# The last 224 rows of w_out: two transfers to sixteen partitions instead of four to eight

## The chip, the cores and the metric

One core of a Trainium2 chip runs the whole program. The metric is the device time of one execution in microseconds (us), as the median of several executions. Executions of one kernel mostly agree within 0.3 us, at most 0.65.

## The reference

For four tokens `x` (4 x 640) it computes `x + A(layernorm(x)) + B(layernorm(x))`. A is attention with a cache of 32 heads and 4096 keys for each token; B is a gated MLP.

```python
q = (xn @ wq)                                  # 640 -> 32 heads x 128
p = softmax(q . k_cache * Dh**-0.5)            # k_cache, v_cache: 4 x 32 x 4096 x 128, bf16
A = (p . v_cache) @ wo                         # 4096 -> 640
z = gelu(xn @ w_in)                            # 640 -> 2 x 864
B = (z1 * (layernorm(z2) * w_sp + b_sp)) @ w_out   # 864 -> 640
```

The two caches are 268 MB of the 282 MB that are read. Each element is used once, so the kernel is a long stream from memory.

## The kernel before

The loads are issued from the sync engine's queue in a fixed order: wq, w_in, the first 640 rows of w_out on 128 partitions, then the last 224 rows of w_out ("the rows" from here on), then units of K and V of 8.39 MB each (K0, K1, ...), and wo last. The rows lie on partitions 0 to 31, seven rows of w_out (8,960 bytes) on each, because the matmul that uses them contracts over those 32 partitions. Where a transfer is called one of "eight rows" or "sixteen rows", a row is what one partition gets: seven rows of w_out, one packet of 8,960 bytes.

```python
wq = at_slot(0, n_q)...;   nc.sync.dma_start(out=wq, in_=A_wq...)          # 5.24 MB
w_in = at_slot(2, n_in)...; nc.sync.dma_start(out=w_in, in_=B_w_in...)      # 2.21 MB
w_out = at_slot(2, FA * NOUT, n_in)...
nc.sync.dma_start(out=w_out, in_=B_w_out[0:nf, :]...)                       # 0.82 MB
w_rest_t = ktpool.tile([P, NKT], F32, tag="kT", name="w_rest")
w_rest = w_rest_t[:32].bitcast(BF16)[:, 0:FR * NOUT].rearrange("p (c n) -> p c n", c=FR)
w_rest_d = B_w_out[nf:Fh, :].rearrange("(i r c) n -> r i c n", r=4, c=FR)
for r in range(4):
    nc.sync.dma_start(out=w_rest[r:32:4], in_=w_rest_d[r])                  # 8 rows, 72 KB
# ... cut ...
load_unit(seq[0])                                                           # K0
```

Transfer r fills partitions r, r + 4, ..., r + 28.

Of the kernel before, what the change touches and what calls it, by code (L numbers as in the profile page):

```python
# [16 lines left out]
def kernel(  # L17
# [19 lines left out]
    nc = tc.nc  # L37
# [18 lines left out]
    Fh = F2 // 2  # L56
    FA = 5
    FR = (Fh - FA * P) // 32
# [56 lines left out]
    nf = FA * P  # L115
# [3 lines left out]
    w_rest = w_rest_t[:32].bitcast(BF16)[:, 0:FR * NOUT].rearrange("p (c n) -> p c n", c=FR)  # L119

    NB = 32 * FC
    z_at = n_in + FA * NOUT
    w_rest_d = B_w_out[nf:Fh, :].rearrange("(i r c) n -> r i c n", r=4, c=FR)
    for r in range(4):
        nc.sync.dma_start(out=w_rest[r:32:4], in_=w_rest_d[r])


    seq = [("k", u) for u in range(B)]
# [212 lines left out]
    for fc in range(FC):  # L341
        n = P if fc < FA else 32
# [248 lines left out]
```

## Time and profile before

| | before |
|---|---|
| median time (first 3 runs) | 664.21 us (664.03 to 664.24) |
| span in the profile | 662.5 us |
| read from memory | 282.25 MB, 426 GB/s over the span |
| K0 complete on all engines | 43.38 us |
| last slice of wo: first and last engine | 654.50 and 658.98 us |

The last two rows come from the completion records in the trace: a transfer over 128 partitions leaves sixteen and each of the four small ones eight. I read that as one from each DMA engine that takes part (K0's first packets start in sixteen streams, at 21.59 to 23.38 us, and K0 leaves sixteen records). The kernel is a stream on sixteen DMA engines that hardly idle (DMA share 1.00 from 30 to 620 us), so the useful question about a load is not "who waits for it" but "which engines does it put back, by how much, and are those the ones that finish last". The prediction shows and reads the lines of the page.

### The profile page before, as it was taken

To read this page: it belongs to the slowest core of one execution; us is meant where nothing else is said; L and a number is where in the kernel's file an instruction comes from. 1 tells how busy PE (TensorE), PEld (TensorE's weight loads), DVE (VectorE), ACT (ScalarE), POOL (GpSimd) and SP (SyncE) were. 2 spreads that over 40 slices of the span, in tenths; PEclk is the share of its full clock that TensorE was granted. 3 is DMA by queue.
4 is the path that set the end of the run, shared out by engine and by line. 5 is a ranking of instruction groups with operands and counts; after the bars stand their busy time and mean duration, and the time that the engine had idled before them with its cause. 6 is when DMAs were issued, how large, how long until landed. Compare 5 with 4: busy or idle time off the path is not lost.

```text
span 662.5 us, 5421 instructions
## 1 busy us (share of the span) xinstructions
PE 292.9 (44%) x2297; PEld 106.5 (16%) x2297; DVE 360.1 (54%) x275; ACT 78.4 (12%) x162; POOL 20.3 (3%) x64
## 2 busy tenths in 40 slices
PE   0636666256072556225336054533506254623245
PEld 0111122112021122111112022111202112211122
DVE  2249899556191759618256286745619185951112
ACT  0300000530100000530200000071010000053200
POOL 6210000000000000000000000000000000000000
PEclk9858768678577587677859596756958759667767
DMA  9999999999999999999999999999999999999996
GB/s 371 463 424 427 426 444 437 435 436 416 443 432 423 439 418 442 433 439 440 423 420 435 432 421 452 433 424 431 431 436 444 428 431 415 445 432 437 418 419 262
DMA packets 6901, 282.61 MB, mean 427 GB/s; under 512 B 808, under 2 KB 1084, under 8 KB 1468
## 3 DMA queue, kind: packets, MB, share of 16 engines
q1 hardware_dynamic: 6856, 282.25, 98.8%
q8 instruction: 18, 0.29, 0.2%
q14 instruction: 7, 0.06, 0.0%
q10 hardware_dynamic: 20, 0.01, 0.0%
HBM read 282.25 MB, written 0.01 MB: 426 GB/s over the span
## 4 chain that ended last, share of the span: by engine, by line
DMA 74%; DVE 11%; issue 11%; PE 2%; ACT 1%; SPq 0%; DVEq 0%; ACTq 0%
DMA kv<-in_A_k_cache_dram 64%; DVE kT L367 11%; DMA kv<-in_A_v_cache_dram 5%; DMA kv<-in_A_wo_dram 3%; DMA kv<-in_A_wq_dram 2%; PE O L449 2%; ACT xd L432 0%; ACT Zb L413 0%; ACT p L421 0%; DVE pT L425 0%; PE last_a L553 0%; DVE m L385 0%; PE S L378 0%; SPq L169 0%; PE misc L390 0%
## 5 line engine op out<-in xcount | busy, mean ns | idle before, releaser
L367 DVE STREAM_TRANSPOSE kT<-kv 128x2048 f32<-128x2048 f32 x128 | 282.8, 2276 | 124.7 <-DMA kv<-in_A_k_cache_dram 124.7
L378 PE MATMUL S<-kT,QZ 128*32 128x512 bf16 x1024 | 187.9, 500 | 230.6 <-DVE kT L367 230.6
L378 PEld LDWEIGHTS <-QZ 128*32 128x32 bf16 x1024 | 60.3, 111 | 353.4 <-issue 332.6
L449 PE MATMUL O<-kv,Zb 128*32 128x512 bf16 x1024 | 73.6, 451 | 58.2 <-DMA kv<-in_A_v_cache_dram 38.0
L458 DVE TENSOR_TENSOR om<-O,Mk 128x512 f32<-128x512 f32 x15 | 10.4, 692 | 109.0 <-PE O L449 109.0
L413 ACT ACTIVATE Zb<-xd,MkE 32x256 bf16<-32x256 bf16 x116 | 52.9, 498 | 110.4 <-PE O L449 109.0
L421 ACT ACTIVATE p<-S,negmax 128x512 bf16<-128x512 f32 x8 | 5.4, 683 | 400.6 <-DVE negmax L399 400.6
L449 PEld LDWEIGHTS <-Zb 128*32 128x32 bf16 x1024 | 32.9, 112 | 97.4 <-issue 55.8
L472 PE MATMUL misc<-R,SelR 128*32 128x128 f32 x32 | 6.4, 281 | 30.0 <-DVE R L459 28.4
L353 POOL COPY QZ<-qT 32x32 bf16<-32x32 bf16 x16 | 5.1, 318 | 390.6 <-PE S L378 389.9
L432 DVE COPY xd<-pT 32x256 bf16<-32x256 bf16 x44 | 16.0, 365 | 0.8
L459 DVE TENSOR_REDUCE R<-om 128x128 f32<-128x512 f32 x15 | 15.3, 1019 | 0.5
L432 ACT COPY xd<-pT 32x256 bf16<-32x256 bf16 x20 | 12.3, 614 | 5.6 <-DVE pT L425 5.2
L425 DVE STREAM_TRANSPOSE pT<-p 128x1024 bf16<-128x1024 bf16 x4 | 5.0, 1245 | 6.3 <-ACT p L421 6.3
L472 PEld LDWEIGHTS misc<-R,SelR 128*32 128x32 f32 x32 | 2.2, 107 | 37.8 <-DVE R L459 26.0
L385 DVE TENSOR_REDUCE m<-S 128x2 f32<-128x1024 f32 x4 | 4.9, 1225 | 5.5 <-PE S L378 5.5
L274 PE MATMUL q<-kv,xnT 128*32 128x512 bf16 x40 | 4.5, 630 | 6.9 <-DMA kv<-in_A_wq_dram 6.9
L461 DVE TENSOR_SCALAR R<-O,Mk 128x128 f32<-128x128 f32 x1 | 0.4, 351 | 12.5 <-PE O L449 12.5
L282 DVE CAST kv<-q 128x512 bf16<-128x512 f32 x1 | 0.7, 692 | 11.1 <-PE q L274 11.1
L390 PE MATMUL misc<-dg,ones_f 128*128 128x256 f32 x8 | 3.2, 488 | 7.6 <-DVE dg L387 7.6
L475 DVE SCALAR_TENSOR_TENSOR om<-misc,rinv,SelH 32x1024 bf16<-32x1024 f32 x4 | 5.1, 1271 | 2.0 <-PE misc L472 2.0
L437 PE MATMUL misc<-rowsum,SelPe 128*32 128x1 f32 x16 | 2.1, 202 | 9.0 <-ACT p L421 9.0
(102 smaller groups left out, 78.2 us busy)
## 6 DMA issues: line engine op xcount, KB each, us to landing
kv<-in_A_k_cache_dram SPq DMA_DIRECT2D x8, 4096.0 KB
kv<-in_A_v_cache_dram SPq DMA_DIRECT2D x1, 6144.0 KB
kv<-in_A_wq_dram SPq DMA_DIRECT2D x1, 5120.0 KB
kv<-in_A_wo_dram SPq DMA_DIRECT2D x3, 1280.0 KB
kv<-in_B_w_in_dram SPq DMA_DIRECT2D x1, 2160.0 KB, 19.9
kv<-in_A_v_cache_dram SPq DMA_DIRECT2D x1, 2048.0 KB
kv<-in_B_w_out_dram SPq DMA_DIRECT2D x1, 800.0 KB
kv<-in_A_wo_dram SPq DMA_DIRECT2D x1, 640.0 KB, 22.0
```

What stands on the lines that cost most here:

```text
L353: nc.gpsimd.tensor_copy(out=QZ[r0:r0 + 32, :, :, :, 8 + 8 * hp], in_=qT[32 * g:32 * g + 32, NE * hp:NE * hp + NE].rearrange("p e a b -> p ...
L367: nc.vector.transpose(kT[:].rearrange("p (t r) -> p t r", r=32), kw)
L378: nc.tensor.matmul(S_ps[32 * q:32 * q + 32, e], lhsT=QZ[:, b, 2 * kh + w, e, w0:w0 + 32], rhs=kb[:, i, :, e, :, w], start=(b == 0 and k < ...
L413: nc.scalar.activation(out=dst, in_=src, func=ACT.Copy, scale=mk)
L421: nc.scalar.activation(out=p_bf[:, :, e, :], in_=S_ps[:, e], func=ACT.Exp, bias=negmax[:, e:e + 1], scale=scale, accum_out=rowsum[:, e:e + 1])
L425: nc.vector.transpose(pT[:].rearrange("p t h x -> p (t h x)"), p_bf[:].rearrange("p t e m -> p (t e m)"))
L432: op(out=xd[32 * hp:32 * hp + 32, :, q, :], in_=pT[32 * q:32 * q + 32, :, hp, :].rearrange("p t x -> p x t"))
L449: nc.tensor.matmul(O_ps[32 * q:32 * q + 32, :, :], lhsT=Zb[b % 2][:, w].rearrange("p h c -> p (h c)"), rhs=vv[:, w * 4 * Dh:(w + 1) * 4 * ...
L458: nc.vector.tensor_tensor(out=om4[:], in0=O_ps[:], in1=Mk4[:, :, None].to_broadcast((P, 4, Dh)), op=ALU.mult)
L459: nc.vector.tensor_reduce(out=R, in_=om4[:].rearrange("p c d -> p d c"), axis=AX.X, op=ALU.add)
L472: nc.tensor.matmul(oh[:], lhsT=SelR[:, b].rearrange("p h b -> p (h b)"), rhs=state["R"][:, b, :], start=(b == 0), stop=(b == B - 1))
L475: nc.vector.scalar_tensor_tensor(out=om[:], in0=oh[:, None, :].to_broadcast((G, HG, Dh)), scalar=state.pop(("rinv", g))[:, 0:1], in1=MkH[: ...
```

## The change

The intent: eight rows use eight of the sixteen engines (eight completion records for each transfer in the trace of before); sixteen rows use all sixteen, and the eight no longer fall behind the others.

```diff
-    w_rest_d = B_w_out[nf:Fh, :].rearrange("(i r c) n -> r i c n", r=4, c=FR)
-    for r in range(4):
-        nc.sync.dma_start(out=w_rest[r:32:4], in_=w_rest_d[r])
+    w_rest_d = B_w_out[nf:Fh, :].rearrange("(i r c) n -> r i c n", r=2, c=FR)
+    for r in range(2):
+        nc.sync.dma_start(out=w_rest[r:32:2], in_=w_rest_d[r])
```

Bytes, rows and their places stay the same. A transfer now fills every second partition instead of every fourth.

## The prediction

What no trace or run of this case shows is cut from the recorded texts, here and under the experiments, and the cuts are marked. The sum of the prediction came to -0.6 us, so to 663.6, all of it from step 2. Between that and the 664.1 to 664.4 of rival (b) the forecast is 663.8. For (b), that a packet takes about twice 0.338 us, the times that follow, and that it is as likely as (a), stand as my estimates. For the range the runs of before (within 0.21 us) and rival (d) remain; the rest of its width is my estimate.

"Lower eight" and "upper eight" are names for the eight engines that carry the rows before the change and the eight that do not; the trace gives no numbers of engines. That the four transfers use the same eight is read from the two groups of K0 starts; that eight-row transfers use these eight in the other runs too is assumed. The order of issue, by the last record of each load: wq 15.92 us, w_in 21.03, w_out 22.93, the rows 23.72, K0 43.38. The completions of all loads fall on eight semaphores, and the fourth piece's eight records (23.28 to 23.72 us) on that of wq.

> **What bounds the kernel now.** I read the page first, then the windows, the DMA queue's waits, the chain of waits, the DMA view of the microseconds that hold the changed transfers, and last the packet records one by one. The page:
>
> ```profile
> DVE  2249899556191759618256286745619185951112
> DMA  9999999999999999999999999999999999999996
> GB/s 371 463 424 427 426 444 437 435 436 416 443 432 423 439 418 442 433 439 440 423 420 435 432 421 452 433 424 431 431 436 444 428 431 415 445 432 437 418 419 262
> ...
> q1 hardware_dynamic: 6856, 282.25, 98.8%
> q8 instruction: 18, 0.29, 0.2%
> ...
> DMA 74%; DVE 11%; issue 11%; PE 2%; ACT 1%; SPq 0%; DVEq 0%; ACTq 0%
> ```
>
> The reader is to see that the DMA row is full in 39 of 40 slices while the fullest compute engine, DVE, has many slices at 1 or 2. One queue (q1) fills 98.8% of the time of sixteen DMA engines with 282.25 MB. The chain names DMA for 74%; its 11% of DVE is the turn in which a finished K unit is transposed before its buffer is reloaded, and it runs while the queue still has other units to move. The windows say this more sharply (their last two figures are DMA share and GB/s):
>
> ```profile
> 2.00:22.00 20.00, 5.74 (x56) 2.36 (x57) 4.58 (x10) 2.05 (x3) 9.04 (x32) 1.00 0.96 410
> 62.00:640.00 578.00, 257.34 (x2020) 93.69 (x2015) 329.63 (x240) 71.01 (x152) 3.91 (x13) 0.73 1.00 432
> 640.00:659.00 19.00, 10.16 (x120) 4.46 (x121) 4.15 (x9) 0.00 (x0) 0.00 (x0) 0.68 0.85 354
> 659.00:662.50 3.50, 0.45 (x4) 0.08 (x1) 0.67 (x2) 0.00 (x0) 0.00 (x0) 0.50 0.01 1
> ```
>
> From 62 to 640 us the share is 1.00. The packet records agree: each 64 KB packet takes 2.418 us, on each engine the next starts at once, and an 8.39 MB unit passes every 19.35 us, while the issue view gives 29.7 us from issue to landing: some 10 us of earlier work is always queued ahead. So the engines are never waited for by themselves, and the end is set by the engine that is furthest behind. From 640 to 659 us the share falls to 0.85 because the engines finish apart: in the records the completions of one transfer are spread over 2.1 us at the first K unit and about 4.5 us at the last slice of wo. The last 3.5 us are matmuls, adds and the store after the last landing.
>
> The part that the change touches is small, but a wait in it is not:
>
> ```profile
> SPq L125 <- DMA kv<-in_A_wq_dram: 11.5, 1, 11.5
> ...
> 0.73 15.19 DMA kv<-in_A_wq_dram
> ...
> 15.94 0.62 SPq L125
> ...
> 16.60 26.78 DMA kv<-in_A_k_cache_dram
> ```
>
> The first line is a wait of the DMA queue, the others are pieces of the chain (start, length). The fourth eight-row transfer cannot be issued until wq has landed at 15.9 us, and the first K unit, K0, waits behind it in program order and is issued at 16.60. The built program tells why: there are eight completion semaphores for these loads, and the fourth piece takes the one that wq still uses.
>
> [...]Eight rows give 8 engines, sixteen give 16. The trace of before agrees: each of these four transfers leaves eight completion records, a 128-row load sixteen; and K0 starts on eight engines at 21.59 to 22.62 us and on the other eight at 22.94 to 23.38. [...]The trace agrees (wq, w_in, w_out, these rows and K0 pass in the order of issue).[...]
>
> **The change part by part.** Removed: two transfers of the four. Bytes, rows and destinations stay: 32 packets of 8,960 bytes, 0.287 MB of 282. No compute instruction changes; what differs on PE, DVE, ACT and GpSimd is numbering of buffers.
>
> 1. Balance. Each packet takes 0.338 us in the records. Before, each of the lower eight engines carries 4, so 4 x 0.338 = 1.35 us; the upper eight carry none. That is just the step between the two groups of K0 starts. After, all sixteen carry 2, 0.68 us. The lower eight come out 0.68 us earlier, the upper eight 0.68 us later.
>
> 2. What this is worth at the end. As no engine idles, a shift at 22 us is carried to 659 us. The other large disturbances are instruction fetches of 16 KB (18 in the page), each of which I see put one engine back by about 1.47 us (at 41.3 us: 1.00 us before the next packet could start and 0.46 us in that packet). At the last slices the completions lie, from the first, at about 2.7 to 2.9, 3.2, then 4.3, 4.4, 4.4 and 4.7 us. The last four fit lower engines hit twice: 1.35 to 1.79 plus 2 x 1.47 gives 4.3 to 4.7. An upper engine hit twice stands at 2.9 to 3.5 (0 to 0.55 plus 2.94). After: lower 3.6 to 4.0, upper 3.6 to 4.2. So the last engine comes 0.5 to 0.7 us sooner, call it 0.6. I cannot follow single engines through the trace with certainty (where two are level they can be swapped), so this attribution is an estimate.
>
> 3. The wait. With two pieces fewer, nothing of this group needs a semaphore in use by wq; K0 needs only the one of the small load of x, which landed at about 3.2 us. So K0 is issued at 3.4 to 4 us rather than 16.60, and the 11.5 us wait goes. Worth: K0's first packet ran at 21.59 us, 5.0 us after its issue, because w_in, w_out and these rows were ahead of it. The early issue only lengthens the queue. K1 still waits for wq's place to be free (the copy of q, at 23.1 us), K2 for K0's transposes. Value 0.
>
> 4. Sequencer: two issues fewer, 2 x 0.62 us, hidden too: 0. The later loads have the same waits with other semaphore numbers, and the consumer of these rows runs at 36.7 us against a landing near 23: 0.
>
> Sum: -0.6 us of 664.21, giving 663.6 if the engines alone set the rate.
>
> **The rivals.**
> (a) Engine-bound, as summed: 663.6. For it: the steady 2.418 us for 64 KB on all engines (27.1 GB/s each) and the exact 1.35 us step.
> (b) [...]a packet takes about twice 0.338 us, the lower eight need 1.35 us as before and the upper eight fall back by 1.35. The slowest (lower, 4.7) stays where it is; upper ones reach 2.9 to 3.5 plus 1.35, about 4.9 at worst. Time 664.1 to 664.4. [...]against it nothing in the trace. I hold this about as likely as (a).
> (c) The 11.5 us wait is on the path, and several us are won: 655 to 660. For it: the chain passes through it (wq, L125, K0). Against it: the 5.0 us that K0's first packet stands queued, and a DMA share of 0.96 in the first window[...]. I give it 1 in 100.
> (d) The engine that ends last is one of the upper eight, or the fetches fall on other engines in the new run: up to 0.7 us slower, or one fetch, 1.5 us, either way. 664.9 to 665.7 at worst.
>
> **Range and chances.** Weighing (a) and (b) equally gives 663.9; with a little for the gain side, because a packet may be shared at less than full contention, I say 663.8. Runs of before agree within 0.21 us[...]. So 663.1 to 664.8. Two per cent would be 13.3 us, which only a form of (c) larger than I can construct would bring: faster 0.01, same 0.985, slower 0.005.
>
> **What would show it right or wrong.** Balance: the step between the two groups of K0 starts vanishes, and the spread of K0's completions falls from 2.1 us to about 1.5 or less (except for a fetch). [...]packets of 8,960 bytes at 0.34 us for (a), at 0.6 to 0.7 us for (b). Wait: the queue's 11.5 us wait at the changed line is gone, the first K issue lies at 3.4 to 4 us, and yet K0 lands within 1 us of 43.4. End: DMA share 1.00 from 62 to 640 us as before, the last landing of wo within 1 us of 659.0. I would be wrong if K0 landed several us earlier, if gaps opened between units, or if a longer queue slowed wq or w_in (wq landing later than 15.9 us).

## The result, and the profile after

The changed kernel takes 665.71 us (665.62 to 665.95, 4 runs) against 664.15 (664.03 to 664.24, 4 runs). The ratio is 1.0024, 95% interval 1.0010 to 1.0038: within 2%, so "same" by that measure, but slower beyond noise.

Where did the 1.6 us come from? First the windows, before and then after (stretch in us, length, busy time and instructions of TensorE, its weight loads, VectorE, ScalarE and GpSimd, then TensorE's clock, DMA share, GB/s):

```profile
2.00:18.00 16.00, 2.39 (x25) 1.22 (x29) 3.69 (x8) 1.47 (x2) 9.04 (x32) 1.00 0.93 397
18.00:30.00 12.00, 8.32 (x52) 2.37 (x44) 3.20 (x5) 4.00 (x5) 2.40 (x6) 0.92 1.06 456
30.00:620.00 590.00, 264.75 (x2038) 95.54 (x2037) 346.64 (x250) 72.43 (x155) 7.42 (x17) 0.72 1.00 433
```

```profile
2.00:18.00 16.00, 2.39 (x25) 1.22 (x29) 3.68 (x8) 1.47 (x2) 9.01 (x32) 1.00 0.93 397
18.00:30.00 12.00, 8.34 (x52) 2.37 (x44) 3.20 (x5) 4.00 (x5) 2.39 (x6) 0.93 1.04 409
30.00:620.00 590.00, 266.06 (x2038) 96.53 (x2037) 346.62 (x250) 72.15 (x154) 7.40 (x17) 0.73 1.00 433
```

Until 18 us and from 30 to 620 us the two move the same: 397 and 433 GB/s. Only in the twelve microseconds that hold the rows does the rate differ, 456 against 409. The DMA share is as high as before (1.04 against 1.06): the engines were busy, they moved less while being busy. (Single windows of a few us are coarse, as a packet of 64 KB counts as a whole; that is why 456 can stand above the long mean.)

Then the chain of work that ended last, after, to set against the one before (start, length, what; SPq is the issuing queue of the sync engine):

```profile
2.21 0.80 SPq L125
...
3.05 0.58 SPq L125
...
3.68 41.02 DMA kv<-in_A_k_cache_dram
```

K0 is issued at 3.68 us instead of 16.60, as predicted. It arrives at 3.68 + 41.02 = 44.70 us instead of 16.60 + 26.78 = 43.38: issued 13 us earlier, landed 1.3 us later. At the other end of the chain, before and after:

```profile
635.85 22.32 DMA kv<-in_A_wo_dram
...
658.65 0.82 PE last_a L553 x4
```

```profile
636.63 23.36 DMA kv<-in_A_wo_dram
...
660.47 0.67 PE last_a L553 x4
```

The slice of wo that the chain ends on lands at 658.17 us before and at 659.99 after. So most of the loss is there at 44 us (1.3 us of 1.8 by the last engine; by the mean over the engines, below, 1.07 of 1.10), and DMA carries it to the end.

The packet records say what happened in between. A page of the profile does not show them one by one:

| | before | after |
|---|---|---|
| 32 packets of 8,960 bytes (the rows) | all 0.338 us | 0.338 to 0.706 us, mean 0.476 |
| first 64 KB packet of K0 on each engine | all 2.418 us | 2.77 to 3.64 us |
| K0 complete: mean over the engines, last engine | 42.33, 43.38 us | 43.40, 44.70 us |
| last slice of wo: mean over the engines, last engine | 657.02, 658.98 us | 658.12, 660.65 us |

Summed over the sixteen engines, the packets of the rows, of the end of w_out and of the start of K0 took 15.8 us more than such packets take undisturbed, 0.99 us for each engine.

### The profile page after: what moved, and what is told of

The parts are those of the page before. It is cut to its first block, busy times and chain, and to the rows that moved or that the text cites. A ratio compares the mean times of both kernels' runs of the same rounds, so it can differ in the third digit from the quotient of the medians.

```text
span 664.0 us, 5419 instructions
## 1 busy us (share of the span) xinstructions
PE 293.7 (44%) x2297; PEld 107.3 (16%) x2297; DVE 360.0 (54%) x275; ACT 78.4 (12%) x162; POOL 20.2 (3%) x64
## 4 chain that ended last, share of the span: by engine, by line
DMA 73%; DVE 11%; issue 11%; PE 2%; ACT 1%; SPq 1%; DVEq 0%; ACTq 0%
DMA kv<-in_A_k_cache_dram 65%; DVE kT L367 11%; DMA kv<-in_A_v_cache_dram 5%; DMA kv<-in_A_wo_dram 4%; PE O L449 2%; ACT xd L432 0%; ACT Zb L413 0%; ACT p L421 0%; SPq L125 0%; DVE pT L425 0%; DVE m L385 0%; PE S L378 0%; SPq L169 0%; PE last_a L553 0%; PE misc L390 0%
## 5 line engine op out<-in xcount | busy, mean ns | idle before, releaser
L378 PE MATMUL S<-kT,QZ 128*32 128x512 bf16 x1024 | 185.2, 494 | 228.5 <-DVE kT L367 228.5
L449 PE MATMUL O<-kv,Zb 128*32 128x512 bf16 x1024 | 77.4, 469 | 61.0 <-DMA kv<-in_A_v_cache_dram 40.8
L449 PEld LDWEIGHTS <-Zb 128*32 128x32 bf16 x1024 | 34.3, 115 | 102.6 <-issue 62.3
```

What stands on the lines that cost most here:

```text
L378: nc.tensor.matmul(S_ps[32 * q:32 * q + 32, e], lhsT=QZ[:, b, 2 * kh + w, e, w0:w0 + 32], rhs=kb[:, i, :, e, :, w], start=(b == 0 and k < ...
L449: nc.tensor.matmul(O_ps[32 * q:32 * q + 32, :, :], lhsT=Zb[b % 2][:, w].rearrange("p h c -> p (h c)"), rhs=vv[:, w * 4 * Dh:(w + 1) * 4 * ...
```

## The experiments

Three theories at the start. **P**: the place decides. Where sixteen engines write to every second of partitions 0 to 31, transfers slow each other (packets of 0.338 to 0.706 us); where eight write to every fourth, they do not (all 0.338 us). By what mechanism, and so which other places should clash, no trace or run of this case shows; what P expects of the runs below stands as my estimate. **W**: issuing K0 13 us earlier, onto a longer queue, is what costs. **S**: a split over sixteen engines of so small a transfer is slow by itself, wherever it goes. For the later runs there is also a question about the end: **L**, the prediction's, that the engines that finish last are lower ones (those that carried the rows before), and **U**, that they are upper ones.

Each kernel ran 4 times. The kernel before was run on the same chip beside each group; its medians were 664.17 to 664.25. "K0" below is the time at which its last engine completed.

### The wait alone: before, without the wait for wq

```diff
-    nc.scalar.dma_start(out=sb_bf[:, 0:1], in_=B_w_sp)
-    nc.scalar.dma_start(out=sb_bf[:, 1:2], in_=B_b_sp[None, :])
+    nc.gpsimd.dma_start(out=sb_bf[:, 0:1], in_=B_w_sp)
+    nc.gpsimd.dma_start(out=sb_bf[:, 1:2], in_=B_b_sp[None, :])
```

> The kernel before with its four eight-row transfers, but the two one-element loads go through GpSimd's queue, so that the fourth piece no longer needs wq's semaphore and K0 is issued at about 5 us. Theory P[...]: nothing changes, 664.15 us within 0.4, all 32 packets of 8960 bytes at 0.338 us, the 11.5 us wait gone. Theory W (issuing K0 13 us earlier, onto a longer queue, is what costs): about 665.7. Theory S (a split over sixteen engines is itself slow, whatever the partitions): 664.15.

Measured: 664.02 us against 664.20, ratio 0.9997 (0.9982 to 1.0012). The chain:

```profile
5.13 38.13 DMA kv<-in_A_k_cache_dram
```

K0 is issued at 5.13 us and lands at 43.26, as before at 43.38. All packets of the rows take 0.338 us. So neither the 11.5 us wait nor the early issue has a price: the transfer stands in the queue instead of the instruction waiting at the issuer.

### The wait put back: the changed kernel, K0 late again

```diff
+    for hf in range(NH):            # moved here from near the end of the program (issued at 581 us)
+        nc.sync.dma_start(out=x_res[32 * hf:32 * hf + B, :], in_=x_flat[:, hf * NO2:(hf + 1) * NO2])
```

> The changed kernel with the wait put back: the two small loads of x_res stand ahead of K0 and take the semaphores of x and wq, so K0 is issued at about 17 us as before the change. Theory P: as the changed kernel, 665.7 within 0.4. Theory W: back to 664.15.

Measured: 665.79 us, ratio 1.0023 (1.0008 to 1.0038).

```profile
16.53 28.32 DMA kv<-in_A_k_cache_dram
```

K0 is issued at 16.53 us, as in the kernel before, and still lands at 44.85. Theory W falls from both sides.

### Sixteen engines over all 128 partitions

```diff
-    for r in range(4):
-        nc.sync.dma_start(out=w_rest[r:32:4], in_=w_rest_d[r])
+    stage = stage_t[:].bitcast(BF16)[:, 0:FR * NOUT // 4]
+    nc.sync.dma_start(out=stage, in_=<the same 224 rows, cut into 128 runs of 2,240 bytes>)
+    nc.gpsimd.memset(w_rest_t[:32], 0.0)
```

The loads over 128 partitions in the kernel before run undisturbed (K0's first packets 2.418 us each), and P expects the same of this one.

> The same 286,720 bytes from the same rows of the source in one transfer to all 128 partitions (2240 bytes each) of another buffer; the matmuls get zeros, so the result is wrong on purpose. [...]K0 is issued early. Theory P: packets as fast as an unshared engine allows (2240 bytes in about 0.09 us), 0.7 us on every engine, spread of K0's starts about 1 us, time 663.0 to 664.3. Theories W and S: about 665.7.

Measured: 664.83 us against 664.20, ratio 1.0009 (0.9992 to 1.0026); the result is wrong as intended. All 128 packets take 0.091 us (8 x 0.091 = 0.73 us on each engine) and K0's first packets 2.418 us: nothing is disturbed, so theory S falls. But the time missed the expected 663.0 to 664.3. This was the first sign that an undisturbed, perfectly balanced transfer gains nothing over the unbalanced one. It seems to lose some 0.6 us: the interval includes 1, but its four runs (664.78 to 664.87) lie above all seven of the kernel before (664.07 to 664.40).

### The same eight engines and rows, other partitions

```diff
-        nc.sync.dma_start(out=w_rest[r:32:4], in_=w_rest_d[r])
+        nc.sync.dma_start(out=stage_t[64 + r:96:4]..., in_=w_rest_d[r])
 # ... later, on ScalarE, which is idle then:
+    nc.scalar.copy(out=w_rest, in_=stage)
```

> The four eight-row transfers of before (same source rows, eight engines, four partitions apart, same waits), but into partitions 64 to 95, with a copy on ScalarE to partitions 0 to 31 that has 10 us to spare. Theory P: [...]packets of 8960 bytes 0.5 to 0.7 us, K0's first packets on the upper engines over 3 us, both groups about 1.3 us later than before: 665.2 to 665.8. Theories W and S: as before, 664.15.

Measured: 665.61 us, ratio 1.0022 (1.0007 to 1.0037). Packets of the rows took 0.338 to 0.705 us (mean 0.561). Seven engines had their first K0 packet stretched to 3.73 to 3.81 us, and the other nine to 2.59 to 3.41. The control is the same kernel with `stage_t[32 + r:64:4]`:

> As the run with partitions 64 to 95, but the four eight-row transfers go to partitions 32 to 63, four apart. [...]Theory P: no contention: 32 packets at 0.338 us, K0's packets at 2.418 us, 664.2 us as before. If only partitions 0 to 31 in this order are free of contention (any other target or buffer disturbs): 665.2 to 665.8 as with partitions 64 to 95.

Measured: 664.20 us against 664.17, ratio 1.0001 (0.9983 to 1.0019), every packet at 0.338 and 2.418 us. The K0 piece of the chain, with partitions 64 to 95 and then with 32 to 63:

```profile
16.72 27.92 DMA kv<-in_A_k_cache_dram
```

```profile
16.80 26.48 DMA kv<-in_A_k_cache_dram
```

The two kernels differ only in the partitions of the spare buffer. Source rows, engines, sizes, order, waits and copy are the same, and K0 lands at 44.64 us with one and 43.28 with the other. What costs is where in SBUF the rows land: 32 partitions further is harmless (packets of 0.338 us, 664.20 us in all) and 64 further is not (up to 0.705 us, 665.61).

### Rows on adjacent partitions

Sixteen adjacent partitions per transfer (changed kernel), then eight adjacent ones (kernel before):

```diff
-    w_rest_d = B_w_out[nf:Fh, :].rearrange("(i r c) n -> r i c n", r=2, c=FR)
-        nc.sync.dma_start(out=w_rest[r:32:2], in_=w_rest_d[r])
+    w_rest_d = B_w_out[nf:Fh, :].rearrange("(r i c) n -> r i c n", r=2, c=FR)
+        nc.sync.dma_start(out=w_rest[16 * r:16 * r + 16], in_=w_rest_d[r])
```

> The changed kernel, but each sixteen-row transfer goes to sixteen adjacent partitions (0 to 15, then 16 to 31)[...]. Theory P: [...]packets of 8960 bytes up to 1.35 us, two of them 2.7 us, against the 1.6 or so of the changed kernel: 666.5 to 667.5. Theories W and S: same as the changed kernel, 665.7.

```diff
-    w_rest_d = B_w_out[nf:Fh, :].rearrange("(i r c) n -> r i c n", r=4, c=FR)
-        nc.sync.dma_start(out=w_rest[r:32:4], in_=w_rest_d[r])
+    w_rest_d = B_w_out[nf:Fh, :].rearrange("(r i c) n -> r i c n", r=4, c=FR)
+        nc.sync.dma_start(out=w_rest[8 * r:8 * r + 8], in_=w_rest_d[r])
```

> The kernel before, but each of its four eight-row transfers goes to eight adjacent partitions[...]. Theory P: [...]each packet of 8960 bytes takes up to 1.35 us, four of them 5.4 us against 1.35: the lower eight engines come out about 4 us late, 667 to 668.5. Theory S (only a split over sixteen engines is slow) and theory W: as before, 664.15.

Measured: 666.26 us (ratio 1.0031, 1.0016 to 1.0046) and 666.05 us (1.0029, 1.0012 to 1.0045). Both are slower, the second although it keeps eight engines, so the number of engines is not the cause. But both missed their size. I had expected packets of up to 1.35 us (4 x 0.338, an estimate); the longest were 0.97 and 0.91 us. And in the second run engines suffered that carried none of the rows: the seven that start K0 first, at 21.64 to 22.14 us (the other nine follow from 23.84 us on), took 3.86 to 3.87 us for that packet, all alike. So the clash is not a neat multiple of 0.338 us, and it reaches engines that carry none of the rows. These runs show which of the places tried clash, and how much; they give no rule for others.

### What the rows cost at all, and who finishes last

Not loaded (zeros instead), then half of them, then half of them twice:

```diff
-    for r in range(4):
-        nc.sync.dma_start(out=w_rest[r:32:4], in_=w_rest_d[r])
+    nc.gpsimd.memset(w_rest_t[:32], 0.0)
```

> The kernel before without these rows: zeros in their place, wrong result on purpose; K0 is issued early. Measures what the rows cost at all. Theory P: the lower eight engines are 1.35 us earlier than before, the upper eight unchanged; 662.8 to 663.7, K0's starts within 1.1 us of each other. Theory W: over 665.

```diff
-    for r in range(4):
+    nc.gpsimd.memset(w_rest_t[:32], 0.0)
+    for r in range(2):
```

> The kernel before with two of its four eight-row transfers, zeros for the rest: wrong result on purpose. The lower eight engines carry 0.68 us instead of 1.35, the upper eight none. Theory U (the engines that end last are two of the upper eight, put back most by instruction fetches; lower ones are level with them only with the full 1.35): 664.2 as before. The prediction's theory L (the last four are lower engines): 0.5 to 0.7 us faster, 663.5.

```diff
     load_unit(seq[0])
+    stage_t = ktpool.tile([P, NKT], F32, tag="kT", name="w_stage")
+    for r in range(2):
+        nc.sync.dma_start(out=stage_t[32 + r:64:4]..., in_=w_rest_d[r])
```

> The kernel before with two of its eight-row transfers issued once more behind K0, into a spare buffer at partitions 32 to 63[...]; right result. The lower eight engines carry 2.03 us instead of 1.35. Theory U: the lower engines, level with the upper ones before, now end last: 0.4 to 0.6 us slower, 664.6 to 664.9. Theory L: 0.68 us slower, 664.9. The end would stay at 664.2 only if the last engines were upper ones with room to spare.

| extra time on lower / upper eight engines | first and last engine at the last slice of wo | time | ratio to before (95%) |
|---|---|---|---|
| 0 / 0 (not loaded) | 654.35, 658.78 | 664.22 | 1.0000 (0.9985 to 1.0015) |
| 0.68 / 0 (half) | 654.52, 659.01 | 664.04 | 0.9998 (0.9982 to 1.0014) |
| 1.35 / 0 (before) | 654.50, 658.98 | 664.17 to 664.25 | |
| 2.03 / 0 (half of it twice) | 654.70, 659.39 | 664.80 | 1.0010 (0.9992 to 1.0028) |
| 0.73 / 0.73 (128 partitions) | 655.34, 659.64 | 664.83 | 1.0009 (0.9992 to 1.0026) |
| 0.68 / 0.68 plus the clash (after) | 656.20, 660.65 | 665.71 | 1.0024 (1.0010 to 1.0038) |

The first of the three missed its 662.8 to 663.7, which was reckoned with L; the second came out as U had it (664.2; L had 663.5); the third cannot tell U (664.6 to 664.9) from L (664.9). The intervals are wide, and all but the last include 1; but the last landings and the times agree, and the runs do not overlap (half of it twice: 664.75 to 664.89, against 664.10 to 664.26 for the kernel before beside it). Load on the lower eight engines alone is free up to the 1.35 us of the kernel before, and costs beyond it. Load on all sixteen costs from the start: 0.73 us on each moves the last landing from 658.78 to 659.64. So L falls and U fits: what finishes last in the kernel before is, or is level with, an upper engine. (This takes for granted that whatever else delays single engines falls alike in these runs; the spread of the last slice fits that, with two stragglers at the end where no rows are loaded, at 4.41 and 4.43 us behind the first engine, and again two in the changed kernel, at 4.20 and 4.45.) The rows had been placed, by luck or by tuning, on engines with time to spare, and without loading them at all (658.78 against 658.98) there would be nothing to win.

Why these engines are late was not tried. With the rows not loaded, the completions of the last slice fall, from the first, into seven engines at 0 to 1.2 us, seven at 2.7 to 3.2 and two at 4.4. The other traffic that visibly puts single engines back is the instruction fetches, 18 of 16 KB and 7 of 8 KB (8 in one run), and the first of them puts one engine back by 1.46 us (1.00 for its own packet and 0.46 in the next). The two stragglers fit engines hit more often, no more than that: the trace does not name an engine.

### A version meant to beat both

```diff
-    FA = 5
+    FA = 6
```

768 rows of w_out on all 128 partitions, and only 96 in the four small transfers.

> A version meant to beat both: 768 rows of w_out in six full chunks over all 128 partitions (FA = 6) and only 96 rows in the four eight-row transfers of before, right result. By theory P the lower eight engines carry 4 packets of 3840 bytes (0.6 us) instead of 1.35, and all carry 0.38 us more of w_out: lower 0.4 us earlier, upper 0.4 later, 663.4 to 664.2; below noise is possible, and where the instruction fetches fall may outweigh it.

Measured: 664.59 us against 664.25, ratio 1.0006 (0.9991 to 1.0021), right result, no packet disturbed. It moves some 0.38 us of work (10,240 bytes more of w_out on each engine, at the 27.1 GB/s of K0's packets: an estimate) from the lower engines to the upper ones, and the last landing is 659.46 instead of 658.98. It missed its 663.4 to 664.2. With U that is what must happen; when I submitted it I still had L in mind. No version tried beats the kernel before beyond noise.

## Why the prediction was wrong

It said 663.8 us, 663.1 to 664.8; the result was 665.71, outside the range and on the other side. That the change stays within 2% was right.

**Right.** DMA-bound with no idle engine: the share is 1.00 and the rate 433 GB/s from 30 to 620 us in both, and a disturbance at 22 us is carried whole (means over the engines: 1.07 us later at K0, 1.10 later at the last slice). Step 3, the wait: K0 issued at 3.68 us, worth nothing, shown from both sides. Strictly, the wait for wq did not vanish; it stands before K1's issue now (11.7 us), where it is as hidden. Step 4, nothing on the compute engines or in the later waits. Rival (c), that several us are won, is out. The balance itself came about: the step between the two groups of K0 starts is gone (fifteen start within 22.17 to 23.22 us, one at 24.23), and wq lands at 15.92 us as before. But two of the prediction's own signs failed: K0 landed 1.32 us later and wo 1.67 us later, and both were to be within 1 us.

**Wrong, step 1, the term "all sixteen carry 2, 0.68 us".** It took the packet's 0.338 us from a trace in which nothing slowed these packets (all 32 took just that). Packets took 0.476 us on average and up to 0.706, and K0's first packets up to 3.64 instead of 2.418. This is the clash that rival (b) had described and that I held "about as likely"; the run with partitions 64 to 95 (packets of up to 0.705 us) and its control with 32 to 63 (all 0.338 us) settle that the place is what matters. Why the places clash they do not show. Even (b) had it too small: it let the clash end with the rows, but the 64 KB packets behind them were caught in it, which is most of the loss (10.9 of the 15.8 us).

**Wrong, step 2, "the last four fit lower engines hit twice".** This attribution turned balance into a gain of 0.6 us. It matched offsets by size alone, and upper engines hit more often give the same offsets (three fetches, 3 x 1.47 = 4.4 us). Two of its readings were also loose: the "exact" step of 1.35 us is the one between the first starts of the two groups (22.94 - 21.59), while their means lie 1.15 us apart; and on the very last slice not four but five engines come late (4.08 to 4.48 us), as one fetch still starts at 656.30 us. The runs with 0, 0.68, 1.35 and 2.03 us on the lower eight show that the end (658.78, 659.01, 658.98 and 659.39 us) does not follow the lower engines until they carry more than they did before. The prediction named this as rival (d), at "up to 0.7 us slower", but did not weigh it in.

**The sum in its place.** The last engine, an upper one by U, now carries two packets that it did not carry before, 2 x 0.338 = 0.68 us, and the clash, 0.99 us on the average engine: 1.67 us. The last landing moved from 658.98 to 660.65, which is 1.67 us. That it agrees to the last digit is partly chance, as the clash differs between engines. By runs rather than by packets: 128 partitions against not loaded gives 0.61 us in time for carrying (664.83 - 664.22), and the changed kernel against 128 partitions 0.88 us for the clash (665.71 - 664.83).

**Still open.** Why some places clash and others do not; why engines that carry none of the rows are slowed in the run with eight adjacent partitions; and which engines the instruction fetches hit.

## What to carry to other kernels

In this stream, which kept all DMA engines busy (share 1.00), spreading a small transfer over all of them was no gain by itself, even undisturbed (664.83 us over 128 partitions against 664.20): ask which engines finish last, and whether the small transfer lies on others. Before raising the number of engines, try where the rows land: eight engines on every fourth of partitions 0 to 31 did better here (664.15 us) than sixteen on every second (665.71). And the packet time of the undisturbed transfer (0.338 us) was not that of the spread one (up to 0.706 us), nor was the damage limited to the transfer that clashed (K0's first packets took 2.77 to 3.64 us instead of 2.418).
